# Second product: 96 stationary columns in place of 128 for the squares' low part on the last 64 output features

## The chip, the cores and the metric

The kernel runs on one core of a Trainium2 chip. The metric is the time of one execution in microseconds of device time; the median of three runs is 2231.03 us (2230.71 to 2231.23). The profile is of one further execution.

The engines are called as in the profile: PE is TensorE's matmuls, PEld its weight loads (in a matmul the stationary operand is loaded into the array first, then the moving operand streams through it, and the sums land in PSUM), DVE is VectorE, ACT is ScalarE, POOL is GpSimd, SP is the engine that issues the DMAs.

## The reference

The input `x` has 8 sequences of 4096 tokens with 192 features. First comes a causal convolution over seven tokens whose weights are a softmax of `weight_gen` for each token and each of 8 heads; then a feed-forward block without biases:

```
w = exp(weight_gen - max);  w = w / (sum(w) + 1e-9)        # over the 7 taps
out[s] = sum over k of w[s, head, k] * x[s + k - 6]         # zeros ahead of the sequence
h = out @ w_in            # 192 -> 2048
r = maximum(h, 0)
g = r * r
y = g @ w_out             # 2048 -> 192
```

All inputs and outputs are fp32.

## The kernel before, in words

The 32768 tokens are worked off in 64 chunks of 512 tokens (`NCH`, `N`). Chunks are pipelined by hand: the main loop runs over chunks `c` and, in each, over eight steps `j`; a step issues the first product of two blocks of 128 hidden features (`mm1`, line 430), the second product of the two blocks of two steps earlier (`pend`, `LAG`, so that the last step of a chunk is worked off in the second step of the next), relu, square and rounding on ScalarE (`relu`, `square`, `high`), the rest on VectorE (`low`, line 459, issued one step late through `late`), and pieces of the convolution of later chunks. The order in which code is issued is the order on each engine.

To reach nearly fp32 accuracy at the matmul rate of a rounded format (fp32r), every operand is split into a high part, which is its rounded value, and a low part, which is the rest. `gh` and `gl` are the two parts of the squares. The weights of the second product lie in `V`, for each of the 16 blocks of hidden features 384 columns: the high parts of the 192 output features in columns 0 to 191, the low parts of the last 64 features in columns 192 to 255, the low parts of the first 128 in columns 256 to 383. So columns 128 to 255 hold the high and then the low parts of the last 64 features.

`mm2_turned` computes the second product of chunks 1 to 62, turned: weights are stationary, the squares of 512 tokens move, output features come out on partitions. For each block it makes five passes. Three (list `A`) go to the first 128 features: high squares on high weights, low squares on high weights, high squares on low weights. Two (list `B`, with `None` in place of a part) go to the last 64 features: high squares and low squares on columns 128 to 255. There the first 64 output partitions collect the products with the high weights, the other 64 those with the low weights; `sum_turned` and `store_turned` add the two halves later. Product of low squares and low weights falls out of the second of these passes as a by-product.

Every pass is two matmuls over 64 rows each, `h` = 0 and 1, which take the lower and the upper 64 hidden features of the block, stand in the two halves of the array's rows, and go to two accumulators (`accs[c][b + h]`). The text calls the two a pair. `mm1` is built of pairs of the same shape. The first and the last chunk, and the transposes at the start, use matmuls over all 128 rows (lines 467, 476 and 329).

Of the kernel before, what the change touches and what calls it, by code (L numbers as in the profile page):

```python
# [21 lines left out]
def kernel(  # L22
# [9 lines left out]
    nc = tc.nc  # L32
    B, S, D = x.shape
# [3 lines left out]
    P = 128  # L37
    Q = 32
# [40 lines left out]
    V = const.tile([P, NF, 2 * D], F32R, name="V")  # L79
# [329 lines left out]
    phs, rgs, ghs, gls, accs = {}, {}, {}, {}, {}  # L409
# [79 lines left out]
    def mm2_turned(c, fb):  # L489
        if fb == 0:  # L490
            accs[c] = [ps_o.tile([P, N], F32, name=f"acc{t}") for t in range(4)]
        gh, gl = ghs.pop((c, fb)), gls.pop((c, fb))
        j, i = divmod(fb, 2)
        first, last = fb == 0, fb == NF - 1
        A, B = [(0, 0, gh), (0, 0, gl), (0, 1, gh)], [(2, None, gh), (2, None, gl)]
        seq = B + A if last or first else A + B
        for n, (b, q, g) in enumerate(seq):
            k = sum(1 for m in seq[:n] if m[0] == b)
            for h in range(2):
                rows = slice(h * D1, (h + 1) * D1)  # L500
                w = V[rows, fb, P:2 * P] if q is None else V[rows, fb, 2 * P * q:2 * P * q + P]
                fl = dict(start=first and k == 0, stop=last and k == (2 if b == 0 else 1))
                nc.tensor.matmul(accs[c][b + h], w, g[rows], **fl)  # L503

    works = {}

# [201 lines left out]
    for c in range(1, NCH):  # L708
        tail = c == NCH - 1
        for j in range(NJ):  # L710
# [11 lines left out]
            if len(pend) == LAG or tail and pend:  # L722
                c2, j2 = pend.pop(0)
                for fb in (2 * j2, 2 * j2 + 1):
                    mm2_turned(c2, fb)
                done = c2 if j2 == NJ - 1 else None
# [23 lines left out]
    c = NCH - 1  # L750
# [54 lines left out]
```

## Time and profile before

| | |
|---|---|
| median of the runs | 2231.03 us |
| profiled execution, span from first to last instruction | 2229.4 us |
| PE busy | 2224.8 us |
| PEld busy | 1846.2 us |
| DVE busy | 1869.8 us |
| ACT busy | 1805.4 us |
| instructions on the core | 50051 |
| matmuls | 19486 |

The profiled execution's own time is known by its span alone; 1.6 us lie between it and the median of the runs. Busy time of PE counts a moment once, however many matmuls overlap in it. Ends of matmuls are modelled in the profile; their starts are recorded. In the timeline, rows that follow each other on one engine from one line are merged, with their count behind an x.

### The profile page before, as it was taken

The numbers are of one execution on the slowest core, as the hardware profiler recorded it, in microseconds if no ns is written. First come the engines' busy times: TensorE is split into PE (matmuls) and PEld (weight loads), VectorE is DVE, ScalarE is ACT, GpSimd is POOL, SyncE is SP. The second block draws the span as 40 slices with busy tenths as digits, with TensorE's granted clock in tenths as the row PEclk, the third lists the DMA queues.
The fourth block names the chain that finished last, engine by engine and source line by source line (L and its number), as shares of the span: only waits on it lengthen the run. The fifth ranks groups of instructions, "written<-read, shape, count | busy, mean of one in ns | idle before, by whom it ended". The sixth has DMA issues, their size and how long they took to land.

```text
span 2229.4 us, 50051 instructions
## 1 busy us (share of the span) xinstructions
PE 2224.8 (100%) x19486; PEld 1846.2 (83%) x19486; DVE 1869.8 (84%) x2866; ACT 1805.4 (81%) x3492; POOL 9.9 (0%) x18
## 2 busy tenths in 40 slices
PE   9999999999999999999999999999999999999999
PEld 8888888888888888888888888888888888888888
DVE  9888888888888888888898888888888888888885
ACT  8888888888888888888888888888888888888886
POOL 0000000000000000000000000000000000000000
PEclk9999999999999999999999999999999999999999
DMA  8433323333233333333332333323333233332322
GB/s 221 96 85 92 90 59 100 83 94 99 57 92 89 88 100 75 74 95 82 100 85 64 100 85 92 88 60 100 84 94 96 54 98 86 91 100 66 82 60 53
DMA packets 323117, 195.30 MB, mean 88 GB/s; under 512 B 223944, under 2 KB 281288, under 8 KB 319040
## 3 DMA queue, kind: packets, MB, share of 16 engines
q1 hardware_dynamic: 321584, 188.58, 33.8%
q0 software_dynamic: 1296, 3.54, 0.9%
q8 instruction: 152, 2.49, 0.5%
q14 instruction: 85, 0.70, 0.1%
HBM read 106.39 MB, written 49.55 MB: 70 GB/s over the span
## 4 chain that ended last, share of the span: by engine, by line
PE 100%; POOL 0%; DVE 0%; issue 0%; POOLq 0%
PE acc L503 50%; PE ph L430 46%; PE acc L467 1%; PE acc L476 1%; PE acc L430 0%; PE acc L341 0%; PE acc L567 0%; PE ph L329 0%; PE ph L770 0%; PE acc L329 0%; PE acc L767 0%; DVE o_sb L773 0%; POOL ident masks.py:199 0%; POOL ident masks.py:197 0%; POOL ex L92 0%
## 5 line engine op out<-in xcount | busy, mean ns | idle before, releaser
L503 PE MATMUL acc<-gh,V 64*128 64x512 f32 x5952 | 1007.4, 386 | 0.0
L430 PE MATMUL ph<-xh,W 64*128 64x512 f32 x6084 | 853.9, 386 | 0.0
L447 ACT ACTIVATE rg<-ph 128x512 f32<-128x512 f32 x992 | 539.1, 597 | 351.5 <-PE ph L430 351.4
L503 PE MATMUL acc<-gl,V 64*128 64x512 f32 x3968 | 772.4, 386 | 0.0
L459 DVE TENSOR_TENSOR gl<-rg,gh 128x512 fp32r<-128x512 f32 x1008 | 644.4, 678 | 139.0 <-ACT gh L455 137.4
L430 PEld LDWEIGHTS ph<-xh,W 64*128 64x128 f32 x6084 | 569.6, 184 | 120.4 <-ACT rg L445 0.4
L503 PEld LDWEIGHTS acc<-gh,V 64*128 64x128 f32 x5952 | 557.5, 184 | 117.1
L451 ACT ACTIVATE rg<-rg 128x512 f32<-128x512 f32 x1008 | 581.3, 633 | 0.2
L455 ACT CAST gh<-rg 128x512 fp32r<-128x512 f32 x1008 | 576.1, 626 | 3.2 <-PE acc L476 3.2
L503 PEld LDWEIGHTS acc<-gl,V 64*128 64x128 f32 x3968 | 371.7, 184 | 78.0
L430 PE MATMUL ph<-xl,W 64*128 64x512 f32 x3042 | 427.3, 386 | 0.0
L266 DVE TENSOR_TENSOR pr<-xt,wt 128x768 f32<-128x768 f32 (+1 forms) x441 | 411.7, 946 | 2.3
L279 DVE TENSOR_TENSOR pr<-pr 128x768 f32<-128x768 f32 x366 | 347.0, 948 | 0.1
L430 PEld LDWEIGHTS ph<-xl,W 64*128 64x128 f32 x3042 | 284.9, 184 | 59.9
L310 DVE TENSOR_TENSOR xl<-xT,xh 128x512 fp32r<-128x512 f32 x186 | 117.7, 688 | 180.9 <-ACT xh L307 180.9
L307 ACT CAST xh<-xT 128x512 fp32r<-128x512 f32 x186 | 102.7, 624 | 0.1
L513 DVE TENSOR_TENSOR raw<-acc,raw 128x512 f32<-128x512 f32 x124 | 79.9, 686 | 5.9 <-ACT raw L511 5.9
L511 ACT COPY raw<-acc 128x512 f32<-128x512 f32 x124 | 66.6, 597 | 0.0
L237 ACT ACTIVATE wt<-wt 128x224 f32<-128x224 f32 x62 | 24.3, 392 | 47.4 <-DVE wt L236 47.4
L393 DVE STREAM_TRANSPOSE xr<-pr 128x768 f32<-128x768 f32 x62 | 60.6, 978 | 2.1
L525 DVE STREAM_TRANSPOSE raw<-raw 64x512 f32<-64x512 f32 x62 | 43.6, 704 | 2.1
L522 DVE STREAM_TRANSPOSE raw<-raw 128x512 f32<-128x512 f32 x62 | 43.7, 704 | 0.0
(93 smaller groups left out, 449.8 us busy)
## 6 DMA issues: line engine op xcount, KB each, us to landing
xT<-xd SPq DMA_DIRECT2D x124, 384.0 KB, 5.0
xt<-in_x_dram SPq DMA_DIRECT2D x30, 1344.0 KB, 6.9
out_dram<-o_sb SPq DMA_DIRECT2D x63, 384.0 KB, 2.7
xd<-xr SPq DMA_DIRECT2D x248, 96.0 KB, 2.0
o_sb<-raw SPq DMA_DIRECT2D x1488, 16.0 KB, 1.8
raw<-raw SPq DMA_DIRECT2D x62, 128.0 KB, 4.2
wt<-in_weight_gen_dram SPq DMA_DIRECT2D x31, 224.0 KB, 3.2
raw<-in_moe_w_in_dram SPq DMA_DIRECT2D x16, 192.0 KB, 5.3
```

The lines of the kernel that those rows point to most:

```text
L266: tt(out=dst, in0=src, in1=wf[:, t0 * H:t1 * H, k:k + 1].broadcast_to([P, m, G]), op=ALU.mult)
L279: tt(out=prs[k0], in0=prs[k0], in1=prs.pop(k), op=ALU.add)
L307: nc.scalar.copy(parts["h"][:, k, n], src[k][:, n])
L310: tt(out=parts["l"][:, k, n], in0=src[k][:, n], in1=parts["h"][:, k, n].bitcast(F32), op=ALU.subtract)
L430: nc.tensor.matmul(two[i], w, xx[rows, k], start=(n == 0), stop=(n == len(seq) - 1))
L447: nc.scalar.activation(r, ph, AF.Relu)
L451: nc.scalar.activation(r, r, AF.Square)
L455: nc.scalar.copy(gh, rgs[c, fb])
L459: nc.vector.tensor_tensor(out=gl, in0=rgs.pop((c, fb)), in1=ghs[c, fb].bitcast(F32), op=ALU.subtract)
L503: nc.tensor.matmul(accs[c][b + h], w, g[rows], **fl)
L511: nc.scalar.copy(X[:, k], acc[b])
L513: nc.vector.tensor_tensor(out=X[:, k], in0=acc[b + 1], in1=X[:, k], op=ALU.add)
```

## The change

In the pass of the low squares to the last 64 features, the stationary operand is cut to columns 128 to 223 of `V` (`P - Q` = 96 columns), and the accumulator to its first 96 partitions. The pass of the high squares keeps 128 columns. So the last 32 low-weight columns are no longer multiplied with the low squares; all that the cut leaves out is part of the by-product of low squares and low weights. In the last of a chunk's 16 blocks the two passes of list `B` change places.

```diff
--- before.py
+++ after.py
@@ -493,14 +493,17 @@
         j, i = divmod(fb, 2)
         first, last = fb == 0, fb == NF - 1
         A, B = [(0, 0, gh), (0, 0, gl), (0, 1, gh)], [(2, None, gh), (2, None, gl)]
+        if last:
+            B.reverse()
         seq = B + A if last or first else A + B
         for n, (b, q, g) in enumerate(seq):
             k = sum(1 for m in seq[:n] if m[0] == b)
             for h in range(2):
                 rows = slice(h * D1, (h + 1) * D1)
-                w = V[rows, fb, P:2 * P] if q is None else V[rows, fb, 2 * P * q:2 * P * q + P]
+                f0 = P if q is None else 2 * P * q
+                n = P if q is not None or g is gh else P - Q
                 fl = dict(start=first and k == 0, stop=last and k == (2 if b == 0 else 1))
-                nc.tensor.matmul(accs[c][b + h], w, g[rows], **fl)
+                nc.tensor.matmul(accs[c][b + h][0:n], V[rows, fb, f0:f0 + n], g[rows], **fl)
 
     works = {}
```

The order on TensorE in any block but a chunk's last, here the end of the second step of chunk 1. `acc2` and `acc3` are the accumulators of the last 64 features, `gh_` and `gl_` the parts of the squares of one block, 128x512 and 96x512 the output. Before:

```order
L503 MATMUL acc2_813<-gh_855,V_87 128x512
L503 MATMUL acc3_814<-gh_855,V_87 128x512
L503 MATMUL acc2_813<-gl_905,V_87 128x512
L503 MATMUL acc3_814<-gl_905,V_87 128x512
L430 MATMUL ph_985<-xh_689,W_86 128x512
```

After:

```order
L506 MATMUL acc2_813<-gh_855,V_87 128x512
L506 MATMUL acc3_814<-gh_855,V_87 128x512
L506 MATMUL acc2_813<-gl_905,V_87 96x512
L506 MATMUL acc3_814<-gl_905,V_87 96x512
L430 MATMUL ph_985<-xh_689,W_86 128x512
```

Nothing moved; the two matmuls of `gl` into `acc2` and `acc3` write 96 partitions.

The order on TensorE over the seam from the second-last to the last block of the same chunk. Before:

```order
L503 MATMUL acc2_813<-gh_1166,V_87 128x512
L503 MATMUL acc3_814<-gh_1166,V_87 128x512
L503 MATMUL acc2_813<-gl_1216,V_87 128x512
L503 MATMUL acc3_814<-gl_1216,V_87 128x512
L503 MATMUL acc2_813<-gh_1168,V_87 128x512
L503 MATMUL acc3_814<-gh_1168,V_87 128x512
L503 MATMUL acc2_813<-gl_1218,V_87 128x512
L503 MATMUL acc3_814<-gl_1218,V_87 128x512
L503 MATMUL acc0_811<-gh_1168,V_87 128x512
L503 MATMUL acc1_812<-gh_1168,V_87 128x512
```

After:

```order
L506 MATMUL acc2_813<-gh_1166,V_87 128x512
L506 MATMUL acc3_814<-gh_1166,V_87 128x512
L506 MATMUL acc2_813<-gl_1216,V_87 96x512
L506 MATMUL acc3_814<-gl_1216,V_87 96x512
L506 MATMUL acc2_813<-gl_1218,V_87 96x512
L506 MATMUL acc3_814<-gl_1218,V_87 96x512
L506 MATMUL acc2_813<-gh_1168,V_87 128x512
L506 MATMUL acc3_814<-gh_1168,V_87 128x512
L506 MATMUL acc0_811<-gh_1168,V_87 128x512
L506 MATMUL acc1_812<-gh_1168,V_87 128x512
```

In the last block the pair of `gl` moved ahead of that of `gh`, and so stands right behind the narrow pair of the block before it.

## Rows read from the trace of the kernel before

**Rows 1.** The page: busy time of the engines, and the chain that ended last.

```profile
PE 2224.8 (100%) x19486; PEld 1846.2 (83%) x19486; DVE 1869.8 (84%) x2866; ACT 1805.4 (81%) x3492; POOL 9.9 (0%) x18
...
PE 100%; POOL 0%; DVE 0%; issue 0%; POOLq 0%
PE acc L503 50%; PE ph L430 46%; PE acc L467 1%; PE acc L476 1%; PE acc L430 0%; PE acc L341 0%; PE acc L567 0%; PE ph L329 0%; PE ph L770 0%; PE acc L329 0%; PE acc L767 0%; DVE o_sb L773 0%; POOL ident masks.py:199 0%; POOL ident masks.py:197 0%; POOL ex L92 0%
```

**Rows 2.** Groups of line 503 and one of line 476, TensorE, shapes kept apart.

```profile
line engine op names shapes xcount | busy us, mean ns | idle before us <-releasers
L503 PE MATMUL acc<-gh,V 64*128 64x512 f32 x5952 | 1007.4, 386 | 0.0
...
L503 PE MATMUL acc<-gl,V 64*128 64x512 f32 x3968 | 772.4, 386 | 0.0
...
L476 PE MATMUL acc<-V,gl 128*128 128x192 f32 x60 | 14.6, 251 | 0.0
```

**Rows 3.** Busy time of the engines from 60 to 2190 us.

```profile
core 0: us, PE busy (x) PEld busy (x) DVE busy (x) ACT busy (x) POOL busy (x), PEclk, DMA share, GB/s
60.00:2190.00 2130.00, 2130.00 (x18798) 1760.38 (x18796) 1794.79 (x2713) 1731.95 (x3344) 4.30 (x5) 1.00 0.34 85
```

**Rows 4.** The chain of waits from 1000 to 1010 us: start, length, matmuls.

```profile
1002.08 2.04 PE ph L430 x18
1004.12 2.27 PE acc L503 x20
```

**Rows 5.** Timeline, a narrow-to-be pair: its weight loads, then its matmuls.

```profile
start us, us, engine line op out<-in xcount [idle before <-releaser]
1001.47 0.19 PEld L503 LDWEIGHTS acc<-gl,V 64*128 64x128 f32 x2
...
1001.69 0.39 PE L503 MATMUL acc<-gl,V 64*128 64x512 f32 x2
```

**Rows 6.** Timeline, from the last pair of the first product into the last product.

```profile
2207.20 0.39 PE L430 MATMUL ph<-xh,W 64*128 64x512 f32 x2
...
2207.51 0.19 PEld L476 LDWEIGHTS acc<-V,gh 128*128 128x128 f32 x1 [0.35 <-issue]
2207.52 0.44 PE L476 MATMUL acc<-V,gh 128*128 128x384 f32 x1
...
2207.62 0.19 PEld L476 LDWEIGHTS acc<-V,gl 128*128 128x128 f32 x1
...
2208.08 0.19 PEld L476 LDWEIGHTS acc<-V,gh 128*128 128x128 f32 x1
...
2208.19 0.19 PEld L476 LDWEIGHTS acc<-V,gl 128*128 128x128 f32 x1
```

**Rows 7.** The transposes at the start: timeline, then their group.

```profile
14.08 1.47 PE L329 MATMUL ph<-ident,wide 128*128 128x128 f32 x12
...
L329 PE MATMUL ph<-ident,wide 128*128 128x128 f32 x16 | 2.1, 272 | 0.0
```

**Rows 8.** The last block of chunk 1: VectorE, then TensorE.

```profile
86.87 1.29 DVE L459 TENSOR_TENSOR gl<-rg,gh 128x512 fp32r<-128x512 f32 x2
...
91.17 0.39 PE L503 MATMUL acc<-gl,V 64*128 64x512 f32 x2
...
92.08 0.39 PE L503 MATMUL acc<-gh,V 64*128 64x512 f32 x2
92.31 0.39 PE L503 MATMUL acc<-gl,V 64*128 64x512 f32 x2
```

## Prediction

> **What bounds the kernel now.** I read the page's busy times first, then its chain, then the chain of one stretch in the middle, then the timeline of single matmuls and weight loads. The page has TensorE's matmul row busy for 2224.8 of 2229.4 us, and the chain that ended last is TensorE to 100%, half of it line 503, the second product [rows 1]. No other engine is in that chain, and the idle time in front of the groups of line 503 is 0.0 [rows 2]. So the time is the sum of the steps at which TensorE starts its matmuls, and an edit counts only if it alters such a step. The granted clock is 1.00 from 60 to 2190 us, the upper of the two levels, 2.4 GHz [rows 3].
>
> The unit is a pair: two matmuls of 64 rows each, one in the upper and one in the lower half of the array, both streaming 512 columns. The chain has 20 matmuls of line 503 in 2.27 us and 18 of line 430 in 2.04 us [rows 4], that is 0.227 us for a pair on either line. Over the whole steady stretch 18,798 matmuls fill 2130.00 us [rows 3]: 2130.00 / 9399 = 226.6 ns a pair. The recorded duration of 386 ns is longer than the step because pairs overlap.
>
> What makes up 226.6 ns? Matmuls of 512 and of 192 columns last 386 and 251 ns [rows 2], 135 ns for 320 columns, 0.42 ns each, about one period of 2.4 GHz. So 512 columns stream for 512 / 2.4 = 213.3 ns, and 13.3 ns of each step are something else. The trace doesn't say what; that is the open term below.
>
> **The change part by part.** Each chunk has 16 blocks, each block two passes of the low part, and one of the two goes to the last 64 features. The trace has 3968 matmuls of the low part on line 503 [rows 2]; half, 1984, lose 32 stationary columns. They are 992 pairs, and at 226.6 ns they take 225 us, a tenth of the span.
>
> *The stream.* The moving operand keeps its 512 columns, and both matmuls of each pair stay. The streamed 213.3 ns is unchanged: 0.
>
> *The weight load.* 128 columns become 96. Two loads that follow each other without a gap in the last product start at 2207.51 and 2207.62, again at 2208.08 and 2208.19 [rows 6]: 0.11 us for 128 columns, 0.86 ns a column. So 96 columns save about 27 ns, over 1984 loads some 54 us of load time. None of it is on the path, if loads stay hidden as now: the load of the pair that starts at 1001.69 starts at 1001.47, with the pair before it, and is over after 0.19 us at 1001.66, 0.03 us early [rows 5]. A shorter load ends earlier still and finds TensorE streaming. The cover is the preceding pair's own step. Value taken: 0. If that cover were gone, the load would show with about the 0.19 us recorded for it, and its shortening would then be a gain on a loss.
>
> *The 13.3 ns of the step.* No row has a stationary operand narrower than 128 columns, so I bound this from both sides. Below: all of it goes, 992 x 13.3 ns = 13.2 us. In between: it is a cost per stationary column, a quarter of it goes, 3.3 ns x 992 = 3.3 us. Above: the array treats 96 columns as another shape; that is priced as a rival. I take 0, nearest to the rows, since the step is the same on both lines with quite different operands and accumulators [rows 4] and looks like a fixed cost of passing from one pair to the next.
>
> *The order in the last block.* In the last block of each of the 62 chunks the low pass now stands ahead of the high pass, so that a full-width pass closes the accumulation. Each pass costs the same step, so the swap moves nothing in the sum. It needs its low part one pair, 0.227 us, earlier. For chunk 1, VectorE writes the last two low parts from 86.87 to 88.16 us, and TensorE's first pass over them starts at 91.17 [rows 8]; the pass of the last block moves from 92.31 to 92.08. A margin of almost 4 us stands in front of it: 0. No DMA and no queue is touched, and nothing is added on ScalarE or VectorE.
>
> Sum: 2229.4 + 0 in the profile. The median of the runs, 2231.03, lies 1.6 us above that span, and I keep this offset: 2231.0 us.
>
> A rule that speaks against the change: in the last product 128 columns load in 0.11 us [rows 6], and the transposes, on plain fp32, start 12 matmuls of 128 columns in a group of 1.47 us; less one duration of 0.27 that is 1.20 / 11 = 0.109 us each, twice what 128 columns need to stream [rows 7]. Both look like loads of one speed. The Trainium skill, "TensorE: Matmul & The Clock Gate", section "Weight-path perf modes", says that a fast weight load is on only when there are exactly 128 weights and the type isn't FP32, and puts it at about twice the speed. By that rule 96 columns would lose a faster path, which gives rival 2; the trace shows no faster path to lose, as the operands here load at the pace of plain fp32.
>
> **The rivals.**
>
> 1. *The gap shrinks* (faster). If the 13.3 ns is time that the load takes from the stream or from the array, fewer columns shorten it. For: the gap exists, and one load per half of the array stands in every step. Against: a load of 110 ns is far larger than the gap, and mostly runs beside the stream. All of it gone gives 2231.0 - 13.2 = 2217.8 us; a share by columns gives 2231.0 - 3.3 = 2227.7 us, which lies within 0.2% and counts as no change.
>
> 2. *The narrow load is slow* (slower). If a column of a narrow load takes double, 96 columns take 165 ns in place of 110 for 128, and the recorded 184 ns become 239. The load starts with the pair before, so it would end 12 ns after the next step is due: 992 x 12 = 12 us, 2243 us. The doubling is my assumption; the loss begins when the load grows by more than the 0.03 us of slack [rows 5]. For: the slack is thin. Against: the evidence of equal speeds above, and the fewer columns.
>
> 3. *A change of shape empties the array* (slower, much). Where the kernel goes from pairs to matmuls over the full array, the last pair starts at 2207.20 and the next weight load at 2207.51, not with that pair; the idle time of 0.35 us before it waits for nothing on record [rows 6]. The stream can start once 0.11 us of load is over, at 2207.62, where a pair would have started at 2207.43: 0.19 us. If going from 128 to 96 columns and back is such a change, each run of narrow pairs costs twice that; there are 15 runs in a chunk, since in the last two blocks two narrow pairs stand together: 62 x 30 x 0.19 = 353 us, 2584 us. Decisive is whether the array is divided differently for 96 columns. Against it: half the array changes with every matmul of a pair without such a stall. The Trainium skill, "TensorEngine Tiling (Array Packing)", section "Key Properties", says that changing the tiling mode drains the engine, which [rows 6] agrees with at 0.19 us; it lists no division of the columns at 96. The same skill, "PSUM — Partial Sum Buffer", section "The four PSUM rules", says that a float32r matmul is always given all four column groups, by which 96 columns would be no other shape; no run here shows that.
>
> 4. *The low part is late in the last block*: 62 waits of at most 0.227 us, 14 us, 2245 us; against it the 4 us of margin.
>
> **How the numbers follow.** No change of the step: 0.52. A quarter of the gap: 0.18. Most or all of it: 0.12. Slow load: 0.09. Change of shape: 0.07. Late low part: 0.02. A measurement of this kernel tells about 0.2%, 4.5 us, from no change: the first two cases are "same" with 0.70, the third is faster with 0.12, the rest slower with 0.18. The predicted time is that of the first, 2231.0 us. The range goes down to 2224, half of the gap, and up to 2243, rival 2, leaving out the full gap below and the change of shape above.
>
> **What would show it.** The timeline of the changed kernel should give the narrow pairs the step of 0.227 us to the pair behind them, and 20 matmuls of the second product in 2.27 us in the chain. The narrow loads should be shorter than 184 ns, by about 27, with more idle time between loads. I am wrong if the step behind a wide load that follows a narrow pair, or into a narrow pair, differs: 0.223 us or less for rival 1, 0.239 for rival 2, 0.4 and idle loads for rival 3. VectorE appearing as a releaser of TensorE at the end of each chunk would be rival 4.

## The result, and the profile after

The changed kernel takes 2257.6 us (2257.47 to 2257.67, four runs) beside 2230.93 us for the kernel before (2230.71 to 2231.23): ratio 1.0119, interval 1.0105 to 1.0134. It is 26.7 us slower, where no change was forecast and the range ended at 2243.

The page of the changed kernel, busy times and the chain that ended last, against [rows 1]:

```profile
PE 2251.0 (100%) x19486; PEld 1821.9 (81%) x19486; DVE 1870.2 (83%) x2866; ACT 1808.2 (80%) x3492; POOL 9.9 (0%) x18
...
PE 100%; DVE 0%; DMA 0%; ACT 0%; issue 0%; DVEq 0%
PE acc L506 51%; PE ph L430 46%; PE acc L467 1%; PE acc L476 1%; PE acc L430 0%; PE acc L341 0%; DMA wt<-in_weight_gen_dram 0%; PE ph L329 0%; PE ph L773 0%; PE acc L329 0%; DVE sm L238 0%; DVE pr L266 0%; DVE mx L235 0%; PE acc L770 0%; DVE o_sb L776 0%; DVE wt L240 0%
```

TensorE is still the whole chain, and its busy time grew from 2224.8 to 2251.0 us, by as much as the span (2229.4 to 2255.7). Nobody makes it wait; its own steps became longer. The groups of the second product on TensorE, now line 506 (columns: busy time, mean of one in ns, idle time before it), against [rows 2]:

```profile
line engine op names shapes xcount | busy us, mean ns | idle before us <-releasers
L506 PE MATMUL acc<-gh,V 64*128 64x512 f32 x5952 | 1005.4, 388 | 0.0
...
L506 PE MATMUL acc<-gl,V 64*128 64x512 f32 x1984 | 389.8, 390 | 0.0
L506 PE MATMUL acc<-gl,V 64*96 64x512 f32 x1984 | 379.6, 389 | 0.0
```

Half of the low part's matmuls are now 96 columns wide, as the change says, and no group has idle time in front. The weight loads of the same two shapes:

```profile
L506 PEld LDWEIGHTS acc<-gl,V 64*128 64x128 f32 x1984 | 185.7, 184 | 41.4
L506 PEld LDWEIGHTS acc<-gl,V 64*96 64x96 f32 x1984 | 159.5, 157 | 44.0
```

The narrow load takes 157 ns in place of 184. The 27 ns are what was forecast; that they cost nothing is what was wrong. The steady stretch, against [rows 3]:

```profile
60.00:2214.00 2154.00, 2154.00 (x18774) 1732.85 (x18772) 1794.26 (x2713) 1732.74 (x3339) 4.30 (x5) 1.00 0.34 84
```

The clock is 1.00 as before; 18,774 matmuls in 2154.00 us make 229.5 ns a pair, where it was 226.6. The chain from 1000 to 1010 us, against [rows 4]:

```profile
1000.34 2.05 PE ph L430 x18
1002.40 2.32 PE acc L506 x20
1004.72 2.05 PE ph L430 x18
1006.77 2.30 PE acc L506 x20
```

Both products lost: 20 matmuls of the second take 2.30 to 2.32 us in place of 2.27, and 18 of the first, whose code is the same, 2.05 in place of 2.04. So the loss isn't in the narrow pairs alone. Single pairs show it. The first step of a chunk on TensorE, in which narrow pairs come second and tenth (x4 are two pairs):

```profile
1002.23 0.39 PE L506 MATMUL acc<-gh,V 64*128 64x512 f32 x2
1002.46 0.39 PE L506 MATMUL acc<-gl,V 64*96 64x512 f32 x2
1002.69 0.40 PE L506 MATMUL acc<-gh,V 64*128 64x512 f32 x2
1002.93 0.40 PE L506 MATMUL acc<-gl,V 64*128 64x512 f32 x2
1003.16 0.62 PE L506 MATMUL acc<-gh,V 64*128 64x512 f32 x4
1003.62 0.39 PE L506 MATMUL acc<-gl,V 64*128 64x512 f32 x2
1003.85 0.63 PE L506 MATMUL acc<-gh,V 64*128 64x512 f32 x4
1004.32 0.40 PE L506 MATMUL acc<-gl,V 64*96 64x512 f32 x2
1004.56 0.85 PE L430 MATMUL ph<-xh,W 64*128 64x512 f32 x6
```

and the first narrow load in it:

```profile
1002.24 0.16 PEld L506 LDWEIGHTS acc<-gl,V 64*96 64x96 f32 x2
```

The narrow load runs from 1002.24 for 0.16 us, and its pair starts at 1002.46, 0.23 us after the pair before. The pairs behind have 128 columns, and still start at 1002.69, 1002.93, 1003.16, 0.23 to 0.24 us apart, where each pair of the kernel before took 0.227 [rows 4]. To see the pattern, the differences between the recorded starts of the first matmuls of successive pairs are listed here in ns, one place of a trace to a line (n marks the step that begins with a narrow or shortened pair, | the return to 226 and 227). They are read from the same records as the timeline:

```
before, in the steady stretch            227 226 227 227 226 227 227 226 227
changed kernel, from 1011.65             230 n230 235 233 236 224 ...
narrow once a step, from 1002.30         230 n230 235 233 236 224 231 236 228 233 231 | 226
before, behind a wait, from 2203.51      240 235 233 236 224 231 236 228 232 231 | 226
```

The sequence is the same in all three. (The line "narrow once a step" is of the second run below.) The kernel before runs on a fixed rhythm, in the text called locked: every pair starts 226 or 227 ns after the one ahead of it. A narrow pair throws it out, and TensorE needs some ten pairs of 224 to 236 ns to fall back. The last line is the point: the trace of the kernel before had the same sequence, behind the few places where its loads came late. There are six, of 4 to 12 steps each; most of the shorter ones are the end of the sequence. The row of weight loads at the last of them, and the matmuls that follow:

```profile
2203.17 0.53 PEld L430 LDWEIGHTS ph<-xh,W 64*128 64x128 f32 x6 [0.41 <-ACT rg L445]
```

```profile
2202.80 1.35 PE L430 MATMUL ph<-xh,W 64*128 64x512 f32 x8
2203.99 0.85 PE L430 MATMUL ph<-xl,W 64*128 64x512 f32 x6
2204.68 1.55 PE L430 MATMUL ph<-xh,W 64*128 64x512 f32 x12
2206.07 0.84 PE L430 MATMUL ph<-xl,W 64*128 64x512 f32 x6
2206.74 0.39 PE L430 MATMUL ph<-xh,W 64*128 64x512 f32 x2
```

From 2204.68 six pairs take 1.39 us, 231.7 ns each, with nothing to wait for and 128 columns throughout; the three from 2206.07 take 0.67. The price of a lost rhythm stood in that trace, in a stretch that the prediction didn't read.

One of the six places shows what is enough to break it:

```profile
18.84 1.07 PE L430 MATMUL acc<-xh,W 64*128 64x512 f32 x8
19.74 0.86 PE L430 MATMUL ph<-xh,W 64*128 64x512 f32 x6
20.44 0.62 PE L430 MATMUL ph<-xl,W 64*128 64x512 f32 x4
```

```profile
19.60 0.57 PEld L430 LDWEIGHTS ph<-xh,W 64*128 64x128 f32 x6
```

The four pairs from 18.84 start 0.227 us apart, the last at 19.52, and the pair at 19.74 starts on time. Only its loads are late: in the locked stretch they start 3 ns behind the pair ahead, here at 19.60, 0.08 us behind it. All widths are full and no matmul waits, yet the steps from 19.74 on are 236 228 232 231 | 227: 20 ns in all. At 23.70 us loads are as late again (steps 233 234 232 228), and the loss is the same 20 ns.

### The profile page after: what moved, and what is told of

Its sections match the earlier page's. It is cut to its first block, busy times and chain, and to the rows that moved or that the text cites. A ratio compares the mean times of both kernels' runs of the same rounds, so it can differ in the third digit from the quotient of the medians.

```text
span 2255.7 us, 50051 instructions
## 1 busy us (share of the span) xinstructions
PE 2251.0 (100%) x19486; PEld 1821.9 (81%) x19486; DVE 1870.2 (83%) x2866; ACT 1808.2 (80%) x3492; POOL 9.9 (0%) x18
## 4 chain that ended last, share of the span: by engine, by line
PE 100%; DVE 0%; DMA 0%; ACT 0%; issue 0%; DVEq 0%
PE acc L506 51%; PE ph L430 46%; PE acc L467 1%; PE acc L476 1%; PE acc L430 0%; PE acc L341 0%; DMA wt<-in_weight_gen_dram 0%; PE ph L329 0%; PE ph L773 0%; PE acc L329 0%; DVE sm L238 0%; DVE pr L266 0%; DVE mx L235 0%; PE acc L770 0%; DVE o_sb L776 0%; DVE wt L240 0%
## 5 line engine op out<-in xcount | busy, mean ns | idle before, releaser
L506 PE MATMUL acc<-gl,V 64*128 64x512 f32 (+1 forms) x3968 | 769.4, 389 | 0.0
L506 PEld LDWEIGHTS acc<-gl,V 64*128 64x128 f32 (+1 forms) x3968 | 345.2, 171 | 85.4
```

The lines of the kernel that those rows point to most:

```text
L506: nc.tensor.matmul(accs[c][b + h][0:n], V[rows, fb, f0:f0 + n], g[rows], **fl)
```

## The experiments

Three theories stood after the comparison: L, a narrow load throws the rhythm out, and the way back has a fixed length; P, each narrow pair has a price; E, each change of width has a price. The edits are shown against the changed kernel. Runs with one narrow or shortened pair a step (line 504 is their second product) leave the swap out; only the first of them shows that in its edit. Edits that narrow or shorten a pass leave work out; they are for timing alone.

**The swap alone.** All passes keep 128 columns; the swap of the two passes in the last block stays.

```diff
-                n = P if q is not None or g is gh else P - Q
+                n = P
```

> All passes keep 128 columns; only the swap of the two passes of the last 64 features in the last block of each chunk stays. Theory L (lock): TensorE's pairs run in a locked rhythm of 226.7 ns; one narrow weight load throws it out, and it takes about 11 pairs and 54 ns in all to fall back, whether or not another narrow load comes in between. Theory P (price): each narrow pair costs 26.9 ns by itself. Theory E (edge): each change between 128 and 96 columns costs 14.3 ns (1860 changes for 26.7 us). All three: no narrow load, 2231 us. If the swap itself were the cause (62 places), 2257 us.

Measured 2230.97 us beside 2230.74, ratio 1.000 (0.9991 to 1.0010). The swap costs nothing; the narrowing costs all.

**One narrow pair a step in place of two.**

```diff
-        if last:
-            B.reverse()
...
-                n = P if q is not None or g is gh else P - Q
+                n = P if q is not None or g is gh or fb % 2 else P - Q
```

> Only blocks with an even number have the narrow pass, one narrow pair in each step in place of two (496 in place of 992), no swap. Theory L: the rhythm is thrown out once a step as before, 496 x 54 ns = 26.7 us, 2257 us. Theory P: half, 496 x 26.9 ns = 13.3 us, 2244 us. Theory E: 992 edges x 14.3 ns = 14.2 us, 2245 us.

Measured 2257.70 us beside 2230.74, ratio 1.0121 (1.0104 to 1.0138). Half as many narrow pairs cost the same: P and E, at 2244 and 2245, fall. One step of this kernel on TensorE, line 504 being the second product:

```profile
1002.30 0.39 PE L504 MATMUL acc<-gh,V 64*128 64x512 f32 x2
1002.53 0.39 PE L504 MATMUL acc<-gl,V 64*96 64x512 f32 x2
1002.76 0.40 PE L504 MATMUL acc<-gh,V 64*128 64x512 f32 x2
1002.99 0.40 PE L504 MATMUL acc<-gl,V 64*128 64x512 f32 x2
1003.23 0.62 PE L504 MATMUL acc<-gh,V 64*128 64x512 f32 x4
1003.68 0.39 PE L504 MATMUL acc<-gl,V 64*128 64x512 f32 x2
1003.92 0.62 PE L504 MATMUL acc<-gh,V 64*128 64x512 f32 x4
1004.38 0.40 PE L504 MATMUL acc<-gl,V 64*128 64x512 f32 x2
1004.61 0.85 PE L430 MATMUL ph<-xh,W 64*128 64x512 f32 x6
```

Only the pair at 1002.53 is narrow. The eight that follow have 128 columns and take 1004.61 - 1002.76 = 1.85 us, 231 ns each. The 19 pairs of a step take 53.3 ns more than 19 locked ones (mean differences of recorded starts, summed), and over all steps 496 x 53.3 = 26.4 us, where the profile lost 26.1 (2255.5 against 2229.4). In the changed kernel the excess is 54.2 ns: its second narrow pair falls into the way back and is nearly free.

**Four narrow pairs a step.**

```diff
-                n = P if q is not None or g is gh else P - Q
+                n = P if g is gh else P - Q
```

> The low squares' pass to the first 128 features is cut to 96 columns too (it leaves out their products with the high weights of features 96 to 127): four narrow pairs a step, 1984 in all. Theory L: the rhythm is out from the first narrow load to some 5 pairs behind the last one, about 14 of 19 pairs at the mean 4.9 ns of the changed kernel, 496 x 69 ns = 34 us, 2265 us, and surely under 2271. Theory P: 1984 x 26.9 = 53.4 us, 2284 us. Theory E: nearly 3900 edges x 14.3 ns = 56 us, 2287 us.

Measured 2273.19 us, ratio 1.0191 (1.0175 to 1.0206): 42.5 us for twice the narrow pairs. P and E asked for 53 to 56, so they miss again; but L had put it "surely under 2271", and that was wrong too. The trace gives 85.0 ns a step on average, but steps are of three kinds. In 364 of the 485 between 60 and 2190 us the rhythm doesn't come back before the next narrow load, and the excess is 93 ns; in the others it comes back, and the excess is 73 or 47. One step of the first kind, from 1013.96; the last nine entries are the first product:

```
230 n230 235 228 n233 234 n232 231 230 n230 235 233 236 224 231 236 228 233 231
```

I had let the rhythm return five pairs behind the last narrow load, as at the end of the long sequence; a narrow load inside the sequence can also throw it back to the sequence's beginning, as the fourth does here.

**All passes of the second product narrow,** but for the first and the last of each accumulator.

```diff
-                n = P if q is not None or g is gh else P - Q
+                n = P if first and k == 0 or last and k == (2 if b == 0 else 1) else P - Q
```

> All five passes of the second product are cut to 96 columns, apart from the first and the last pass of each accumulator in a chunk (it leaves out a quarter of the second product): 4712 narrow pairs. The first product keeps 128 columns. Theory L: narrow pairs among themselves may lock again, so the cost is at the changes from one product to the other, at most 2 x 54 ns a step, 0 to 53 us, 2231 to 2284 us, and steps of one constant length inside the second product. Theory P: 4712 x 26.9 = 127 us, 2358 us. Theory E: about 1240 edges x 14.3 ns = 18 us, 2249 us.

Measured 2263.44 us, ratio 1.0147 (1.0131 to 1.0162). 4712 narrow pairs cost 32.7 us, 7 ns each, so P's price per narrow pair is out of the question; E's 18 us is too little. The time lies in L's wide range, but the constant steps that L had hoped for came in another form. Narrow pairs among themselves take 231, 229, 229 and 231 ns in turn: of 2501 stretches of four such steps between 60 and 2190 us, 2497 take 920 ns. That is a rhythm of their own, of 230.0 ns a pair, 3.3 slower than the locked 226.7; and the first product behind them needs its way back.

**Other widths,** once a step in the same place: 112, 126 and 64 columns, and 120 after these were measured.

```diff
-                n = P if q is not None or g is gh else P - Q
+                n = P if q is not None or g is gh or fb % 2 else 112
```

> One pass a step (even blocks, low squares, last 64 features) keeps 112 of 128 columns, no swap. Theory L (any departure throws the rhythm out, and falling back costs 53 ns a step): 2257 us, as with 96. Theory D (cost in proportion to the missing columns): 16 in place of 32, 13 us, 2244 us.

> The same pass keeps 126 of 128 columns, so that its load is about 2 ns shorter. Theory L in its strict form (any departure): 2257 us. If the rhythm holds against a small departure: 2231 us. Theory D: 1.7 us, 2232.5 us. If what counts is whether there are exactly 128 columns: 2257 us.

> The same pass keeps 64 of 128 columns; the program then gives these matmuls an array divided into 64 x 64 in place of 64 x 128. Rival 3 of the prediction, here a change of shape for certain: 2 x 496 changes at 0.19 us, 188 us, 2419 us, with idle time before the narrow loads. Theory L without a price for the shape: 2257 us. Theory D: 53 us, 2284 us.

> One pass a step (even blocks, low squares, last 64 features) keeps 120 columns. So far the excess over a locked step of 226.7 ns was, in each step of 19 pairs, 53.3 ns at 96 columns, 20.0 at 112 and at 64, 6.7 at 126: 8, 3 and 1 times 6.67 ns. Theory G (the rhythm falls back only on a grid of 6.67 ns): the excess is again such a multiple, most likely 1 or 3 of them, 3.3 or 9.9 us, 2234 or 2241 us. Theory D (proportion to missing columns, 53.3 x 8 / 32): 13.3 ns, 6.6 us, 2237.5 us.

| columns | time, us | before beside it | ratio | excess a step, ns (trace) | in units of 6.67 ns |
|---|---|---|---|---|---|
| 126 | 2234.35 | 2230.89 | 1.0016 (1.0006 to 1.0026) | 6.7 | 1 |
| 120 | 2234.45 | 2231.09 | 1.0016 (1.0007 to 1.0025) | 6.7 | 1 |
| 112 | 2241.19 | 2230.89 | 1.0046 (1.0031 to 1.0061) | 20.0 | 3 |
| 96 | 2257.70 | 2230.74 | 1.0121 (1.0104 to 1.0138) | 53.3 | 8 |
| 64 | 2240.80 | 2230.89 | 1.0045 (1.0030 to 1.0060) | 20.0 | 3 |

Every width costs, even 126, so L holds in kind, but its 2257 us for 112, 126 and 64 was missed each time, and the size has no order: 64 columns are cheaper than 96. Cost in proportion to the missing columns (D) falls with that. The steps, from the step into the narrow pair on:

```
126 columns    233 n227 | 227
120 columns    234 n226 | 227
112 columns    226 n236 228 232 231 | 227
 64 columns    226 n236 228 233 231 | 226
 96 columns    230 n230 235 233 236 224 231 236 228 233 231 | 226
```

112 and 64 columns enter the same sequence near its end; 126 and 120 pay one long step and are back. What was expected for 120 by theory G, a multiple of 6.67 ns, came true; D's 13.3 ns didn't.

The run with 64 columns answers rival 3 as well. Its group of narrow loads, and a narrow pair with the two behind it:

```profile
L504 PEld LDWEIGHTS acc<-gl,V 64*64 64x64 f32 x992 | 66.6, 131 | 19.5
```

```profile
1005.04 0.40 PE L504 MATMUL acc<-gl,V 64*64 64x512 f32 x2
1005.27 0.39 PE L504 MATMUL acc<-gh,V 64*128 64x512 f32 x2
1005.50 0.40 PE L504 MATMUL acc<-gl,V 64*128 64x512 f32 x2
```

The program divides the array into 64 x 64 for these matmuls and into 64 x 128 for their neighbours, and nothing empties: the pair behind the narrow one at 1005.04 starts at 1005.27. A drain of 0.19 us at each change would have been 188 us; 9.9 us came. The Trainium skill, "TensorEngine Tiling (Array Packing)", section "Key Properties", says that changing the tiling mode drains the engine. [Rows 6] agree for the passage from 64 to 128 rows, at 0.19 us; for this change of columns under equal rows the run disagrees, and the measurement decides.

**The moving operand shortened in place of the load,** by 16 tokens and, after that was measured, by 8.

```diff
-                nc.tensor.matmul(accs[c][b + h][0:n], V[rows, fb, f0:f0 + n], g[rows], **fl)
+                nc.tensor.matmul(accs[c][b + h][:, 0:n], V[rows, fb, f0:f0 + P], g[rows, 0:n], **fl)
```

Here `n` is 496 or 504 in the same pass, once a step, and 512 elsewhere.

> All loads have 128 columns; in place of that, the same pass streams 496 of its 512 tokens (it leaves out 16 tokens of the low squares' part). 496 pairs stream 6.7 ns less, 3.3 us in all. Theory L, if any departure of a pair throws the rhythm out: 2231 - 3.3 + 26 = 2254 us, with steps of 230 to 236 behind the short pairs. If only the weight loads count: 2227.7 us, with one step of 220 ns and the others at 226.7.

> All loads 128 columns wide; the same pass streams 504 of 512 tokens (it leaves out 8 tokens of the low squares' part), 3.33 ns less, half of the grid of 6.67 ns (496 took off exactly one). Theory G: the pair falls between two places of the grid, so it doesn't gain 3.33 ns for good: either the step stays 226.7, 2231 us, or the rhythm is thrown out, 3 to 8 grid units a step, 2241 to 2257 us. If only loads can throw it out: 496 x 3.33 ns = 1.7 us less, 2229.3 us.

With 496 the time was 2227.81 us beside 2230.89, ratio 0.9986 (0.9977 to 0.9995): 3.1 us less, the 3.3 of the shorter stream (work left out, not a better kernel). The rhythm held:

```profile
1003.76 0.38 PE L504 MATMUL acc<-gl,V 64*128 64x496 f32 x2
1003.98 0.39 PE L504 MATMUL acc<-gh,V 64*128 64x512 f32 x2
1004.21 0.39 PE L504 MATMUL acc<-gl,V 64*128 64x512 f32 x2
```

One step of 0.22 us from 1003.76, then 0.23 again. So it looked as if loads alone could throw the rhythm out. The run with 504 says no: 2254.30 us beside 2231.09, ratio 1.0104 (1.0090 to 1.0118). Less work than before, loads of 128 columns throughout, and 23.2 us more:

```profile
1000.99 0.39 PE L504 MATMUL acc<-gh,V 64*128 64x512 f32 x2
1001.21 0.39 PE L504 MATMUL acc<-gl,V 64*128 64x504 f32 x2
1001.44 0.40 PE L504 MATMUL acc<-gh,V 64*128 64x512 f32 x2
1001.67 0.39 PE L504 MATMUL acc<-gl,V 64*128 64x512 f32 x2
1001.90 0.63 PE L504 MATMUL acc<-gh,V 64*128 64x512 f32 x4
```

Its steps from 1001.21 on are n224 233 232 233 236 223 232 236 228 232 231 | 227, the known sequence; the excess over a step is 46.7 ns, seven units.

16 columns at 2.4 GHz are 6.67 ns, 8 columns half of that, and the locked step of 226.67 ns is 34 x 6.67. In these two runs a pair could become shorter by a whole unit, and not by half a unit. That was one of the two branches of theory G's expectation, within its 2241 to 2257.

**Only the first matmul of the pair narrow.**

```diff
-                n = P if q is not None or g is gh else P - Q
+                n = P if q is not None or g is gh or fb % 2 or h else P - Q
```

> 96 columns once a step as in the run with one narrow pair a step, but only in the first matmul of the pair; the second keeps 128. If the load that ends early throws out its own half of the array, or the start of the next load: 2257 us as before. If what counts is when the later of the two loads ends: no change, 2231 us. Half of the disturbance: 2244 us.

Measured 2257.55 us, ratio 1.0119 (1.0105 to 1.0132): the whole loss from one narrow matmul and load of two. The trace shows more than was asked:

```profile
1001.72 0.39 PE L430 MATMUL ph<-xh,W 64*128 64x512 f32 x1
1001.73 0.39 PE L504 MATMUL acc<-gh,V 64*128 64x512 f32 x1
```

Rows with x1 are single matmuls. At 1001.72 and 1001.73 one of the first product and one of the second start together, 0.01 us apart: the halves of the array, which start 3 ns apart in every locked pair, are a whole pair apart here.

**All passes of the second product 112 wide.** The edit is that of all-narrow, with 112.

```diff
-                n = P if q is not None or g is gh else P - Q
+                n = P if first and k == 0 or last and k == (2 if b == 0 else 1) else 112
```

> All passes of the second product keep 112 columns, apart from the first and last of each accumulator in a chunk (it leaves out an eighth of the second product): 4712 narrow pairs; with 96 columns the same took 2263 us, with steps of 229 to 232 and no lock. Theory L: with 112 the disturbance of one pair was 3 grid units in place of 8; if the narrow pairs find a lock of their own at 226.7, only the passage between the products costs, about 20 ns twice a step, 2251 us or less. A price per narrow pair (20 ns each): 2231 + 94 = 2325 us. If the 13.3 ns that a step takes beyond its 512 columns were a cost by stationary columns, narrow steps would be 1.7 ns shorter: 2231 - 8 = 2223 us.

Measured 2253.59 us, ratio 1.0100 (1.0085 to 1.0115), 22.5 us for 4712 narrow pairs. The price per narrow pair, 94 us, and the gap that shrinks with the columns are both out. L's 2251 or less was missed by 2.6. The narrow pairs have a rhythm of their own again, but not at 226.7: their steps are 229, 232 and 226 ns in turn, 687 ns for three (685 to 688 in 2751 of 2999 such stretches), 229 a pair. The expectation's "no lock" for 96 columns was wrong as well: the run above has its stretches of 920 ns.

No run points to a kernel faster than the one before: it is locked nearly everywhere, with 0.8 us lost in the six places, the waits themselves included (excess of its recorded steps over 226.67, summed).

## Why the prediction was wrong

- *What bounds the kernel* was right: TensorE to 100% before and after, so an edit counts by the step between pairs.
- *The stream* (0) was right.
- *The weight load* is the step that failed. The prediction said "A shorter load ends earlier still and finds TensorE streaming", value 0. The load did shrink by 27 ns, 184 to 157, and was hidden; but the step of 226.7 ns was not a sum of independent costs. It was a rhythm of loads and streams together, which a pair of another width breaks, here at 53 ns for the first narrow pair of a step and over the next ten pairs. The term, put at 0, measures 496 x 54.2 = 26.9 us.
- *The 13.3 ns* was read as "a fixed cost of passing from one pair to the next" and bounded above only by a change of shape. The bound that was missing is the one in the trace of before: four to twelve steps of 224 to 240 ns in six places.
- *The order in the last block* (0) was right: 2230.97 us with the swap alone.
- *Rival 1*, the gap shrinks: false; with 4712 pairs at 96 or 112 columns the steps grew.
- *Rival 2*, slow narrow loads: false, although the sign was right. Recorded loads take 184 ns at 128 columns, 157 at 96 and 131 at 64, 0.83 ns a column all the way. The rule of the Trainium skill on the fast weight load ("TensorE: Matmul & The Clock Gate", section "Weight-path perf modes"), by which 128 columns would be a faster case unless the type counts as FP32, isn't seen in these loads.
- *Rival 3*, a change of shape: false; with 96 columns the steps at the narrow pair are 230 ns, not 400, and even the real change to 64 x 64 cost 9.9 us in all.
- *Rival 4*: false; no engine stands as a releaser in front of line 506.
- The sign that the prediction named, a step that differs "behind a wide load that follows a narrow pair, or into a narrow pair", appeared with 230 ns on both, between the marks for rival 1 and rival 2; most of the loss lies further behind, where it named nothing.

Shown: the rhythm, its loss by a pair of another width, by a stream of 504 or by a load that only starts late (19.60 us in the trace of before), and the way back along one sequence. A second narrow pair on that way is nearly free (53.3 ns for one a step, 54.2 for two), but not every further one is: four cost 85.0. Open: what on the chip sets the unit of 6.67 ns, and why 96 columns enter the sequence eight units from its end while 64 and 112 enter three from it. Load and matmul have one width here, so a narrow load with a full matmul wasn't tried; the long step into the narrow pair at 96, 120 and 126 columns lies ahead of any narrow matmul, but at 64 and 112 the first long step is behind it.

## What to carry to other kernels

When an engine runs a long stretch at one exact step, take the regularity itself as something that an edit can break: look in the trace for places where it was broken already, behind a wait, and read what falling back costs. A change that makes one instruction in a stream smaller isn't bounded by zero because it is hidden. Test such an edit with fewer and with more places: a cost that doesn't scale with their number belongs to the disturbance, not to the instruction.

## What the runs showed of the hardware that was not expected

- Pairs of 64-row matmuls with 512 moving columns, each with its own load of 128 columns, lock at 226.67 ns; out of the lock they take 223 to 240, some 231 on average, and come back in up to twelve steps along one sequence.
- The excess of a single disturbance came in multiples of 6.67 ns: 1 (126 and 120 columns), 3 (112 and 64), 8 (96), 7 (504 moving columns). 496 moving columns took exactly one unit off. Single steps are no multiples; their sums are.
- Dividing the columns of the array differently, 64 x 64 between 64 x 128, cost 20 ns a time, no more than 112 columns under the same division.
- A load of full width that started 0.08 us late, ahead of a pair that started on time, cost three units.
- Narrow pairs among themselves run in a rhythm of their own: 920 ns for four pairs at 96 columns, 687 for three at 112.
- One narrow load and matmul in one half of the array cost the same as in both (2257.55 and 2257.70 us), and let the halves drift apart.
